# Attention, routed experts and a summed MLP on one core: the sum steps re-spaced, a buffer of its own for the last weights, row turnings inside a y, idle turnings at branches

## Chip, cores and metric

One core of one Trainium2 chip runs the whole program in one launch. The metric is the device time in microseconds (us); the kernel before has a median of 1106.93 us over 3 runs (1106.44 to 1108.24).

## What is computed

Three stages follow each other, all in float32. Each large product is made as three products of a high and a low part (hi·hi, hi·lo, lo·hi).

```python
def reference(**kwargs):
    attn_out = _attn_ref(**attn_kwargs)              # softmax inside chunks of 64
    x = ...reshape(B * S, H * D)                     # 4608 tokens x 512
    x = _moe_ref(x=x, **moe_kwargs)
    return _moe2_ref(x=x, **moe2_kwargs)

# _moe_ref: a token with x @ w_skip > 0 goes to the expert e_idx = argmax(x @ w_gate):
    h = np.maximum(xc[mask] @ w1[e], 0.0)            # 512 -> 1024
    y[mask] = gate_w[mask, None] * (h @ w2[e])       # 1024 -> 512
    out[do_compute] = xc + y

# _moe2_ref: on all tokens
    h = np.maximum(np.maximum(x @ w1, x @ w2), x @ w3)   # 512 -> 768, three times
    return (h @ w_out).astype(np.float32)
```

The weights of the last MLP come in 64-bit words and are narrowed on the chip.

## The kernel before

**Stages.** Attention and routing fill the first 225 us or so. Then come the eight experts `e0` to `e7`, about 225 to 530 us, and then the second MLP in five blocks of tokens (block 0 from about 530 to 660 us, the others to the end).

**An expert.** Tokens are gathered in tiles of 128. `first_tiles` does two tiles together: four groups of `h` products on TensorE (PE), each followed by a high part `hhi` on ScalarE (ACT) and a low part `hlo` on VectorE (DVE), then transposes `trm` of rows that are needed later (ACT writes `xhi`, DVE writes `xlo`), and two `second` calls, whose 24 `y` products each end in `put_back`: DVE adds to `xg` (L694) and GpSimd (POOL) scatters the rows into `x_dram` (L696). A third tile is done by `single`, under a branch on the expert's count (L983); a fourth one stands under a further branch (L916), and more of them in a loop (L920, L921). Expert 0 always does its third tile, and expert 7 does its own (`7_2`) after the branch of L989, before the second MLP. Every engine takes each branch for itself, in its own order of instructions. Where a branch is not taken, the engine makes up the semaphore counts that the skipped instructions would have given, and it does so only after its own earlier work; the others wait for those counts. In the profiled run the branches of `e2`, `e3` and `e5` are taken, and inside them the fourth-tile branches of `e2` and `e3`; those of `e1`, `e4`, `e6` and `e7` are not taken, and neither are the ones after `0_2` and `5_2` and the loops after `2_3` and `3_3`.

**Expert weights.** While expert e runs, the weights of e+1 are loaded on SyncE's queue (SP), split by ACT (`whi_e`) and DVE or POOL (`wlo_e`), and the pieces numbered 6, 4 and 5 are split after the branch.

**Sum steps.** The second MLP uses sums of quarters of its weights in the manner of Strassen, seven products in place of eight. 18 `sums_ahead` steps (#0 to #17) make these sums: 11 of them among the experts, 7 in block 0. A step loads `n_raw`, narrows it into `n_q` (DVE L531, L532, L533, L536, and a square on ACT, L534), forms four sums (DVE L569 to L572), makes the high part on ACT (L575) and the low part on DVE (L576), and stores both to `m_sums` (L577 on ACT's queue, L578 on SP's). Among the experts `n_q` has one buffer, so the next step's first instructions on DVE and ACT wait until the last store has landed. `STEPS` says how many steps stand in each expert: 2, 2, 2, 2, 2, 1, 0, 0. In `first_tiles` they are bound to the first and second group of `h`; in expert 0 they come after the third tile's rows have been turned.

**The seam.** `single("7_2")` calls `sums_T(0, 0)` ahead of its y products. It turns the x rows of block 0 (PE `trf`, L879), which ACT and DVE make into `x_b` and `t` (L884, L885, L890, L893 to L900). These rows are loaded at the start of that stage by `load_first`, on SP, behind every scatter.

**Block 0.** `unit` does seven products of six matmuls each (`f_a`, `f_b`, `f_d`); ACT copies some to `p` and `u`, DVE adds and takes maxima (L1034, L1036, L1056). Each of the first seven of the nine units carries a sum step, and the units 6, 7 and 8 each narrow two halves of the last weights (`m2_direct`, tiles `raw_m` and `n_q_m`, five DVE instructions each). `n_q_m` takes turns with the steps' `n_q` in the two buffers of the tag `s4`. A later unit reads a step's stored sums through `ws` loads (L851).

**Order.** Tile's scheduler sets the order on each engine. It follows the order of the code, dependencies, and `issue_after`, which holds an instruction back in the order behind another one.

## Time and profile before

| what | value |
|---|---|
| median of 3 runs | 1106.93 us (1106.44 to 1108.24) |
| the profiled execution's own time | 1109.83 us |
| its span | 1108.1 us |
| PE busy | 1042.2 us, 94% |
| DVE busy | 614.8 us, 55% |
| ACT busy | 446.2 us, 40% |
| POOL busy | 309.1 us, 28% |
| mean granted clock of PE | 0.979 |

The profiled execution is 2.9 us above the median, and 1.7 us of it lie outside the span. Times in rows count from the span's start. A granted clock of 1.00 is 2.4 GHz and 0.50 is 1.2 GHz. In a timeline, a row's bracket holds the idle time before the instruction and what ended it. A releaser with a q (`DVEq`, `PEq`) is that engine's sequencer: here the counts that it makes up at a branch.

### The profile page before, as it was taken

How to read it: one execution, taken by the hardware profiler on the slowest of the kernel's cores; microseconds unless marked ns; L12 is line 12 of the kernel's file. 1: busy time of each engine (PE TensorE's matmuls, PEld its weight loads, DVE VectorE, ACT ScalarE, POOL GpSimd, SP SyncE). 2: the span in 40 equal slices, each digit the busy share in tenths (PEclk: the TensorE clock that was granted, in tenths of full speed). 3: DMA queues.
4: the chain of work that ended last, by engine and by line, in shares of the span. 5: the costliest groups of instructions: out<-in, count | busy, mean ns of one | idle time of the engine just before them, and what ended most of it. 6: DMA issues, size and time to landing. Idle time of an engine off the chain costs nothing.

```text
span 1108.1 us, 17499 instructions
## 1 busy us (share of the span) xinstructions
PE 1042.2 (94%) x6320; PEld 872.1 (79%) x6320; DVE 614.8 (55%) x1299; ACT 446.2 (40%) x774; POOL 309.1 (28%) x297
## 2 busy tenths in 40 slices
PE   7899799988899998998899799999999999999997
PEld 6788677777788787887687588878888888788996
DVE  6687588756756477671499772335244442443241
ACT  6677487434434244431444342222322232223231
POOL 4124232364404044320432160222312140123021
PEclk9999799999899999999999999999999999999999
DMA  9999996257764468544898934663566545666591
GB/s 211 195 216 232 261 229 183 89 195 259 265 217 136 138 211 273 192 150 141 274 319 285 300 114 136 197 190 114 165 194 192 166 139 166 183 186 208 186 288 38
DMA packets 217513, 216.99 MB, mean 196 GB/s; under 512 B 50219, under 2 KB 179403, under 8 KB 217408
## 3 DMA queue, kind: packets, MB, share of 16 engines
q1 hardware_dynamic: 206384, 183.62, 57.3%
q0 software_dynamic: 8432, 23.76, 6.6%
q10 hardware_dynamic: 2592, 8.26, 1.9%
q8 instruction: 60, 0.98, 0.4%
q14 instruction: 45, 0.37, 0.1%
HBM read 175.15 MB, written 41.83 MB: 196 GB/s over the span
## 4 chain that ended last, share of the span: by engine, by line
PE 41%; DMA 6%; DVE 3%; issue 3%; POOL 1%; ACT 0%; SPq 0%; POOLq 0%; DVEq 0%; ACTq 0%
PE f_a L705 5%; PE f_a L707 5%; PE f_a L706 5%; PE o L705 4%; PE o L707 4%; PE o L706 4%; DMA ws<-m_sums 3%; PE f_d L705 3%; PE f_d L707 3%; PE f_d L706 3%; DMA m_sums<-n_q 2%; PE f_b L705 1%; PE f_b L707 1%; PE f_b L706 1%; PE trf L879 1%
## 5 line engine op out<-in xcount | busy, mean ns | idle before, releaser
L91 POOL TENSOR_TENSOR fh<-best,fh 128x512 fp32r<-128x512 f32 (+1 forms) x60 | 77.0, 1290 | 356.3 <-ACT fh L90 270.4
L705 PE MATMUL f_a<-x_t,ws 128*128 128x512 f32 (+1 forms) x270 | 100.7, 373 | 5.0 <-DVE p L1034 4.8
L706 PE MATMUL f_a<-x_t,ws 128*128 128x512 f32 (+1 forms) x270 | 99.9, 370 | 0.0
L707 PE MATMUL f_a<-x_t,ws 128*128 128x512 f32 (+1 forms) x270 | 99.7, 370 | 0.0
L90 ACT CAST whi_e<-raw_e 128x1024 fp32r<-128x1024 f32 x64 | 65.1, 1045 | 60.0 <-DMA raw_e<-in_moe_w_dram 34.8
L705 PE MATMUL h<-xhi,whi_e 128*128 128x256 f32 x256 | 75.5, 295 | 12.2 <-DVEq L983 7.0
L706 PE MATMUL o<-wlo_m,fh 128*128 128x512 f32 x216 | 84.6, 392 | 0.0
L705 PE MATMUL o<-whi_m,fh 128*128 128x512 f32 x216 | 83.4, 392 | 0.0
L707 PE MATMUL o<-whi_m,fh 128*128 128x512 f32 x216 | 83.4, 392 | 0.0
L91 DVE TENSOR_TENSOR wlo_e<-raw_e,whi_e 128x1024 fp32r<-128x1024 f32 x50 | 67.1, 1351 | 18.1 <-ACT whi_e L90 15.9
L705 PE MATMUL y<-whi_e,hhi 128*128 128x512 f32 x184 | 74.3, 406 | 2.6 <-ACT hhi L772 1.8
L707 PE MATMUL y<-whi_e,hlo 128*128 128x512 f32 x184 | 72.8, 400 | 1.8 <-DVE hlo L712 1.6
L706 PE MATMUL h<-xlo,whi_e 128*128 128x256 f32 x256 | 74.4, 291 | 0.0
L707 PE MATMUL h<-xhi,wlo_e 128*128 128x256 f32 x256 | 74.3, 290 | 0.0
L706 PE MATMUL y<-wlo_e,hhi 128*128 128x512 f32 x184 | 72.3, 395 | 0.0
L696 POOL DMA_INDIRECT x_dram<-xg,ids_sb x20 | 20.6, 1030 | 180.2 <-DVE xg L694 72.8
L90 ACT CAST fh<-best 128x512 fp32r<-128x512 f32 (+1 forms) x60 | 34.7, 579 | 89.5 <-DVE best L1036 57.9
L1039 ACT COPY p<-f_a 128x512 f32<-128x512 f32 (+1 forms) x45 | 24.5, 545 | 99.3 <-PE f_a L707 99.1
L705 PEld LDWEIGHTS h<-xhi,whi_e 128*128 128x128 f32 x256 | 51.0, 199 | 15.3 <-ACTq L983 6.3
L705 PEld LDWEIGHTS f_a<-x_t,ws 128*128 128x128 f32 x270 | 51.2, 190 | 14.5 <-DVE p L1034 5.3
L707 PEld LDWEIGHTS f_a<-x_t,ws 128*128 128x128 f32 x270 | 51.2, 190 | 8.6
L706 PEld LDWEIGHTS f_a<-x_t,ws 128*128 128x128 f32 x270 | 51.2, 190 | 8.3
(226 smaller groups left out, 2678.7 us busy)
## 6 DMA issues: line engine op xcount, KB each, us to landing
ws<-m_sums SPq DMA_DIRECT2D x135, 512.0 KB, 5.2
raw_e<-in_moe_w_dram SPq DMA_DIRECT2D x64, 512.0 KB, 5.1
ws<-m_sums SPq DMA_DIRECT2D x45, 256.0 KB, 3.9
v_bd<-in_v_dram SPq DMA_DIRECT2D x144, 64.0 KB, 4.2
x<-x_dram SPq DMA_DIRECT2D x36, 256.0 KB, 4.9
out_dram<-os SPq DMA_DIRECT2D x36, 256.0 KB, 2.0
x_dram<-xg SPq DMA_DIRECT2D x17, 512.0 KB, 4.2
m_sums<-n_raw ACTq DMA_DIRECT2D x18, 448.0 KB, 6.0
```

The lines of the kernel that those rows point to most:

```text
L90: nc.scalar.copy(hi, src),
L91: eng.tensor_tensor(lo, src, hi.bitcast(F32), op=ALU.subtract),
L696: ins = nc.gpsimd.indirect_dma_start(out=x_dram[:, :], out_offset=bass.IndirectOffsetOnAxis(ap=ids, axis=0), in_=xg, in_offset=None, bound ...
L705: nc.tensor.matmul(acc, ahi, bhi, start=first, stop=False, skip_group_check=onto)
L706: nc.tensor.matmul(acc, ahi, blo, start=False, stop=False, skip_group_check=onto)
L707: return nc.tensor.matmul(acc, alo, bhi, start=False, stop=last, skip_group_check=onto)
L879: nc.tensor.transpose(tr[:, i * P:(i + 1) * P], row[:, c * P:(c + 1) * P], ident)
L1039: nc.scalar.copy(p1, acc_a)
```

## The change

It has four parts.

1. Sum steps: `STEPS` becomes 1, 2, 2, 2, 2, 2, 0, 0, and the two steps of an expert are bound to the first and the third group of `h` in place of the first and the second.
2. Own buffer: `n_q_m` gets a buffer of its own (4 KB per partition), and the first half piece of the last weights goes from unit 6 to unit 3 (`SPREAD`).
3. Seam: `sums_T(0, 0)` is placed behind the third group of the last y (nine of its 24 products). Inside `sums_T`, the split of b22 stands ahead of t2 and t3.
4. Idle turnings: `second` issues eight 128x128 transposes of the identity, into a tile `busy` that nobody reads, behind the last y of a branch's predecessor: after `first_tiles` of e1 to e7, and after every `single` but `7_2`.

```diff
-    def second(name, key, hhi, hlo, i, xg, ids, tag=None):
+    def second(name, key, hhi, hlo, i, xg, ids, tag=None, inside=None, ahead_of_branch=False):
...
-                mm3(acc, hhi[:, kf, sl], hlo[:, kf, sl], bhi[:, kf % 2, :], blo[:, kf % 2, :], n == 0, n == 7)
+                done = mm3(acc, hhi[:, kf, sl], hlo[:, kf, sl], bhi[:, kf % 2, :], blo[:, kf % 2, :], n == 0, n == 7)
+            if inside and n == 2:
+                with tc.issue_after(done.ins):
+                    inside()
+        if ahead_of_branch:
+            busy = ps_tr(f"busy_{name}")
+            with tc.issue_after(done.ins):
+                for n in range(8):
+                    nc.tensor.transpose(busy[:, n % 4 * P:n % 4 * P + P], ident, ident)
         put_back(key, xg, ids, acc)
...
-            if n % 2 == 2 - per and side:
+            if n in (0, 4) and side:
                 with tc.issue_after(done[0].ins), tc.issue_after(done[1].ins):
                     side.pop(0)()
...
-            second(f"{name}_{i}", (e, i), hhi, hlo, i, xgs[i], idss[i], "tr" if e == 0 else None)
+            second(f"{name}_{i}", (e, i), hhi, hlo, i, xgs[i], idss[i], "tr" if e == 0 else None,
+                ahead_of_branch=e > 0 and i == 1)
...
-        second(name, key, hhi, hlo, 0, xg, ids)
+        second(name, key, hhi, hlo, 0, xg, ids, inside=inside, ahead_of_branch=inside is None)
...
-    STEPS = [2, 2, 2, 2, 2, 1, 0, 0]
+    STEPS = [1, 2, 2, 2, 2, 2, 0, 0]
...
-        quarters = four_kb([P, 8, P], F32, f"n_q_m{m}_{f}_{half}", True)
+        quarters = fpool.tile([P, 8, P], F32, tag="n_q_m", name=f"n_q_m{m}_{f}_{half}", bufs=1)
...
         tr22 = turned(cc + 2, 1)
+        split_x("b22", tr22, nc.vector)
         nc.vector.tensor_tensor(t2, tr22, t1, op=ALU.subtract)
         nc.vector.tensor_tensor(t3, tr22, b12, op=ALU.subtract)
-        split_x("b22", tr22, nc.vector)
...
-                single(f"{e}_2", (e, 2), *third, lambda: sums_T(0, 0))
+                single(f"{e}_2", (e, 2), *third, inside=lambda: sums_T(0, 0))
...
+        SPREAD = [0, 0, 0, 1, 0, 0, 1, 2, 2]
...
-                if b == 0 and 3 * f + m >= 6:
-                    for _ in range(min(2, len(rest))):
-                        rest.pop(0)()
+                for _ in range(SPREAD[3 * f + m] if b == 0 else 0):
+                    rest.pop(0)()
```

In the order that is built, DVE reaches the branch after `0_2` (L916 before, L925 now) straight behind `put_back`'s add; the three instructions L531 to L533 of step #1 that stood there before are now in expert 1.

**Place 1: DVE in expert 1, from the first group's `hlo` on.** `n_q_3965` (before) and `n_q_4583` (now) are step #1, `n_q_4572` and `n_q_4653` step #2, `hlo` is one group's low part each, `wlo_e` a piece of the next expert's weights. Before:

```order
L712 SCALAR_TENSOR_TENSOR hlo_4542<-h_0_4543,hhi_4541 128x512
L572 TENSOR_TENSOR n_q_3965<-n_q_3965 128x128
L712 SCALAR_TENSOR_TENSOR hlo_4542<-h_2_4586,hhi_4541 128x512
L91 TENSOR_TENSOR wlo_e_2_4526<-raw_e_2_4523,whi_e_2_4525 128x1024
L576 TENSOR_TENSOR n_q_3965<-n_q_3965,n_raw_3963 128x896
L712 SCALAR_TENSOR_TENSOR hlo_4542<-h_4_4629,hhi_4541 128x512
L91 TENSOR_TENSOR wlo_e_3_4532<-raw_e_3_4529,whi_e_3_4531 128x1024
L712 SCALAR_TENSOR_TENSOR hlo_4542<-h_6_4656,hhi_4541 128x512
```

Now:

```order
L712 SCALAR_TENSOR_TENSOR hlo_4553<-h_4_4624,hhi_4552 128x512
L571 TENSOR_TENSOR n_q_4583<-n_q_4583 128x128
L572 TENSOR_TENSOR n_q_4583<-n_q_4583 128x128
L91 TENSOR_TENSOR wlo_e_3_4543<-raw_e_3_4540,whi_e_3_4542 128x1024
L712 SCALAR_TENSOR_TENSOR hlo_4553<-h_6_4667,hhi_4552 128x512
L576 TENSOR_TENSOR n_q_4583<-n_q_4583,n_raw_4581 128x896
L518 TENSOR_TENSOR xlo_2_4701<-trm_2_0_4702,xhi_2_4700 128x512
```

The low part of step #1 (L576), whose store frees `n_q`, stood ahead of the third group's `hlo` and now stands behind the fourth's. Step #2 follows it in both, behind three `xlo`, and the branch (L983, now L992) behind step #2.

**Place 2: PE at the last y, `7_2`.** `y_2` is its product, `trf_0_1` and `trf_0_0` are the first turnings of block 0's rows. Before:

```order
L770 MATMUL trh_2_0_8229<-ident,h_2_0s 128x128 x4
L705 MATMUL y_2_8278<-whi_e_7_7251,hhi_2_8190 128x512
L706 MATMUL y_2_8278<-wlo_e_7_7252,hhi_2_8190 128x512
L879 MATMUL trf_0_1_8239<-ident,x_1_8173 128x128
L879 MATMUL trf_0_0_8245<-ident,x_0_8172 128x128 x4
L707 MATMUL y_2_8278<-whi_e_7_7251,hlo_2_8191 128x512
```

Now:

```order
L779 MATMUL trh_2_0_8508<-ident,h_2_0s 128x128 x4
L705 MATMUL y_2_8515<-whi_e_7_7458,hhi_2_8469 128x512
L706 MATMUL y_2_8515<-wlo_e_7_7459,hhi_2_8469 128x512
L707 MATMUL y_2_8515<-whi_e_7_7458,hlo_2_8470 128x512
...
L707 MATMUL y_2_8515<-whi_e_6_7964,hlo_2_8470 128x512
L888 MATMUL trf_0_1_8528<-ident,x_1_8452 128x128
L888 MATMUL trf_0_0_8534<-ident,x_0_8451 128x128 x4
L705 MATMUL y_2_8515<-whi_e_6_7964,hhi_2_8469 128x512
```

The five turnings stood behind two of the 24 products of `y_2` and now stand behind nine. Further on, six matmuls of `f` that stood behind the turnings `trf_1_0` now stand ahead of them.

**Place 3: DVE in block 0, between unit 5 and unit 6.** `n_q_8921` (before) and `n_q_9212` (now) are the last sum step, #17; `n_q_m_0_0` and `n_q_m_0_1` are the first two half pieces of the last weights; `best` is the running maximum. Before:

```order
L1034 TENSOR_TENSOR best_0_2_1_8911<-u_0_0_2_8908,f_0_2_d 128x512
L571 TENSOR_TENSOR n_q_8921<-n_q_8921 128x128
L1056 TENSOR_TENSOR best_0_1_2_8655<-best_0_1_2_8655,f_2_1_a 128x512
L572 TENSOR_TENSOR n_q_8921<-n_q_8921 128x128
L531 TENSOR_SCALAR n_q_m_0_0_8981<-raw_m_0_0_8979 128x512
L576 TENSOR_TENSOR n_q_8921<-n_q_8921,n_raw_8825 128x896
```

Now:

```order
L572 TENSOR_TENSOR n_q_9212<-n_q_9212 128x128
L1043 TENSOR_TENSOR p_0_2_1_9108<-p_0_2_1_9108,f_2_1_a 128x512
L1045 TENSOR_TENSOR best_0_1_3_8935<-best_0_1_3_8935,p_0_2_1_9108 128x512
L531 TENSOR_SCALAR n_q_m_0_1_9270<-raw_m_0_1_9268 128x512
L576 TENSOR_TENSOR n_q_9212<-n_q_9212,n_raw_9116 128x896
L1043 TENSOR_TENSOR best_0_2_0_9201<-p_0_0_2_9198,f_0_2_b 128x512
```

The last step's low part (L576) stood behind three sums of unit 6 and behind the first narrowing into a shared buffer. It now stands ahead of unit 6's sums, and the narrowing ahead of it writes into a buffer of its own; the first half piece has gone further up, among unit 4's sums.

## Rows read from the trace of the kernel before

**Rows 1.** The page's part 1: busy us, share of the span, instructions.

```profile
PE 1042.2 (94%) x6320; PEld 872.1 (79%) x6320; DVE 614.8 (55%) x1299; ACT 446.2 (40%) x774; POOL 309.1 (28%) x297
```

**Rows 2.** PE's waits from 225 us on: us in total, times, longest us.

```profile
PE h L705 <- DVEq L983: 7.0, 3, 3.8
...
PE y L707 <- DVE hlo L712: 1.6, 1, 1.6
...
PE h L705 <- PEq L920: 0.8, 1, 0.8
...
PE h L705 <- PEq L916: 0.5, 1, 0.5
```

**Rows 3.** Stretches: start:end, length, PE busy (matmuls), granted clock, DMA share, GB/s.

```profile
262.54:265.95 3.41, 3.41 (x18) 0.50 0.26 78
289.84:296.67 6.83, 6.08 (x28) 0.50 0.98 311
440.03:443.44 3.41, 2.94 (x7) 0.50 1.00 358
521.95:525.36 3.41, 3.41 (x11) 0.50 1.04 342
535.60:539.01 3.41, 3.41 (x12) 0.50 0.18 57
620.94:624.35 3.41, 2.93 (x6) 0.50 0.86 253
0.00:18.00 18.00, 11.52 (x85) 1.00 0.93 217
```

**Rows 4.** Timeline of PE at the branch after `0_2`: start, length, instruction, idle before.

```profile
261.30 0.39 PE L705 MATMUL h<-xhi,whi_e 128*128 128x256 f32 x1 [2.81 <-ACTq L916]
```

**Rows 5.** Timeline of ACT at the same place.

```profile
260.14 0.67 ACT L534 ACTIVATE n_q<-n_raw 128x512 f32<-128x512 f32 x1 [6.07 <-DMA m_sums<-n_q]
```

**Rows 6.** Timeline of DVE in expert 1.

```profile
273.30 1.08 DVE L576 TENSOR_TENSOR n_q<-n_q,n_raw 128x896 fp32r<-128x896 f32 x1
...
283.19 0.43 DVE L531 TENSOR_SCALAR n_q<-n_raw 128x512 int32<-128x512 int32 x1 [1.61 <-DMA m_sums<-n_q]
...
289.52 0.74 DVE L694 SCALAR_TENSOR_TENSOR xg<-y,xg 128x512 f32<-128x512 f32 x1
```

**Rows 7.** The tile `m_sums` from 225 to 530 us: its transfers.

```profile
DMA to landing us min/median/max: 2.5/6.8/9.1
```

**Rows 8.** Timeline of PE in expert 2: transposes, and the taken branch L983.

```profile
304.84 1.47 PE L514 MATMUL trm<-ident,xg 128*128 128x128 f32 x12
...
317.06 0.39 PE L705 MATMUL h<-whi_e,xhi 128*128 128x512 f32 x1
```

**Rows 9.** Timeline of DVE at the start of expert 5.

```profile
426.34 0.43 DVE L531 TENSOR_SCALAR n_q<-n_raw 128x512 int32<-128x512 int32 x1 [6.28 <-DMA m_sums<-n_q]
```

**Rows 10.** Timeline of PE at the seam.

```profile
521.90 1.27 PE L879 MATMUL trf<-ident,x 128*128 128x128 f32 x5 [1.39 <-DMA x<-x_dram]
...
534.35 0.63 PE L879 MATMUL trf<-ident,x 128*128 128x128 f32 x4 [2.16 <-DVE x_b L885]
...
546.13 0.33 PE L879 MATMUL trf<-ident,x 128*128 128x128 f32 x1 [1.16 <-DMA x<-x_dram]
```

**Rows 11.** Timeline of PE in block 0, at its two gaps.

```profile
621.34 0.80 PE L705 MATMUL f_a<-x_t,ws 128*128 128x512 f32 x1 [4.84 <-DVE p L1034]
...
626.07 0.50 PE L705 MATMUL f_a<-x_b,ws 128*128 128x512 f32 x1 [1.80 <-DMA ws<-m_sums]
```

**Rows 12.** Timeline of DVE ahead of these gaps.

```profile
613.15 1.55 DVE L531 TENSOR_SCALAR n_q_m<-raw_m 128x512 int32<-128x512 int32 x1 [1.90 <-DMA m_sums<-n_q]
614.62 1.08 DVE L576 TENSOR_TENSOR n_q<-n_q,n_raw 128x896 fp32r<-128x896 f32 x1
...
617.14 0.69 DVE L536 SCALAR_TENSOR_TENSOR n_q_m<-n_q_m 128x512 f32<-128x512 f32 x1
```

**Rows 13.** A stretch of block 0: PE, PEld, DVE, ACT, POOL busy, granted clock, DMA.

```profile
580.00:600.00 20.00, 20.00 (x90) 16.57 (x89) 18.54 (x33) 8.24 (x14) 6.18 (x8) 1.00 0.88 306
```

More of the change, by code (lines that the diff above doesn't have):

```diff
@@ L748, in first_tiles, with single @@
         for i in range(2):
-            second(f"{name}_{i}", (e, i), hhi, hlo, i, xgs[i], idss[i], "tr" if e == 0 else None)
+            second(f"{name}_{i}", (e, i), hhi, hlo, i, xgs[i], idss[i], "tr" if e == 0 else None,
+                ahead_of_branch=e > 0 and i == 1)
         return hhi, hlo
-    def single(name, key, xT, xg, ids, between=None):
+    def single(name, key, xT, xg, ids, between=None, inside=None):
         e = key[0]
@@ L1059 @@
         rest = [lambda i=i, half=half: m2_direct(3, i, wpool2, half) for i in range(NS) for half in range(2)]
+        SPREAD = [0, 0, 0, 1, 0, 0, 1, 2, 2]
     else:
         rest = [lambda i=i: m2_piece(3, i, wpool2) for i in range(NS)]
+        SPREAD = [0, 0, 0, 0, 0, 0, 1, 1, 1]
     steps = list(range(AHEAD, 2 * len(UNITS)))
```

## Prediction

> **What bounds the kernel now.** I read the busy times first. TensorE (PE) is busy 94% of the span, VectorE (DVE) 55% [rows 1], so the time is PE's work plus PE's idle time, and nothing else counts unless it opens or closes a gap of PE. The second view is therefore PE's waits from the experts on [rows 2]. There the reader sees branches (`DVEq`, `ACTq`, `PEq`: another engine, or PE itself, comes late to a branch) and some late inputs. Third come the stretches in which PE's granted clock is 0.50, so 1.2 GHz [rows 3]. Each follows an idle time of PE: 2.81 us ahead of the one at 262.54, 1.64 ahead of 440.03, 1.39 ahead of 521.95, 2.16 ahead of 535.60, 4.84 ahead of 620.94. What such a stretch costs: at full clock 90 products of 512 columns take 20.00 us, 0.222 each [rows 13]; at 0.50 seven take 2.94 and six 2.93 [rows 3], 0.42 to 0.49. So a stretch loses 7 × 0.20 = 1.4 to 6 × 0.27 = 1.6 us; the 18 half-wide products at 262.54 lose 3.41 − 18 × 0.111 = 1.4 us. A stretch goes if the gap ahead of it goes: 1.80 us [rows 11] and the 0.8 of the `PEq` gaps [rows 2] have none of their own behind them.
>
> **A. Expert 0 to 2: sum steps.** At the branch after `0_2`, PE waits 2.81 us for ACT's counts [rows 4]; ACT stood 6.07 us in front of step #1's square, until step #0's store had landed [rows 5]. That square is gone from there. What is late next is PE itself: eight turnings and its own drain. Twelve transposes take 1.47 us with the latency of the last in it [rows 8], at most 0.12 each; I take 0.11, so eight are 0.88 us; the drain is 0.5 to 0.8 [rows 2]. The gap becomes about 0.88 + 0.7 = 1.6, a gain of 1.2.
> Expert 1 pays for it. Before, it runs from 261.30 to the `DVEq` gap's end at about 290.6, 29.3 us: L576 of step #1 starts at 12.0 and lasts 1.1, step #2 starts 8.8 later when the store has landed, and DVE is done with it and the last `xg` add 7.1 later, at 290.3 [rows 6]. Now L576 stands behind the fourth `hlo`. With h at full clock (96 half-wide products, 10.7 us) and some 2.2 us for the high part and the cast (an estimate from the other casts' and adds' lengths of 0.7 to 1.1 in these rows) it starts at 12.9. With a landing of 6.8, the median of such stores [rows 7], expert 1 lasts 12.9 + 1.1 + 6.8 + 0.2 + 7.1 + 0.3 = 28.4, a gain of 0.9; with the 8.8 that was seen here 30.4, a loss of 1.1; with 2.5, PE's own end decides, 24.2 of products and 1.6 behind them, a gain of 3.5. I take 0.9, the median. Its stretch at half clock brings nothing more, since DVE sets the end. A = 1.2 + 0.9 = **2.1**, between 0.1 and 4.7.
>
> **B. Expert 5.** DVE stood 6.28 us in front of step #8, which was first in its queue [rows 9]; the pieces of the weights and all `hlo` came late behind it, and PE waited 1.6 us for one of them [rows 2] and ran seven products at half clock behind it (1.4). Step #8 now stands behind the weight pieces and the first `hlo`, so the store has 5 us or more to land beside PE's work. B = **3.0**, its upper end; the lower one is 1.6, if only the wait goes.
>
> **C. Experts 4 and 6.** The branches there wait 7.0 − 3.8 = 3.2 us for DVE in two cases [rows 2]. The last step's low part now stands behind the last `xg` add, in front of the branch, in both; its length is 1.1 us [rows 6]. I take 0.5 for each, as about half of it lies beside the turnings (0.88). C = **−1.0**, between 0 and −4.5 (each gap longer by 1.5, with a half-clock stretch of 1.4 behind one).
>
> **D. Idle turnings.** They run at 13 places of this execution: seven branches after `first_tiles`, and after `0_2`, `2_2`, `2_3`, `3_2`, `3_3` and `5_2`. At the five taken branches PE goes on without a gap (the first product behind the branch of expert 2, at 317.06, has no idle time ahead of it) [rows 8], so each pays 0.88: 4.4. Where PE waits for its own sequencer (0.8 and 0.5) [rows 2] the drain follows the turnings: 2 × 0.88 = 1.8. Behind `3_3` PE waits for the `xg` add, which is 0.7 long [rows 6] and runs beside the turnings; I take 0.5, between 0.2 and 0.9. The others hide in gaps that another engine ends, or are in A. D = **−6.7**; ends: −4.4, if only the taken ones pay, and −11.4, if all 13 do.
> On the clock: the first 18 us of the run, which begin with eleven idle transposes and are mostly transposes of q and k, show 1.00 [rows 3].
> The Trainium skill ("TensorE: Matmul & The Clock Gate", Part 4, PE-mode transpose) says that transposes don't count as PE being busy in the way matmuls do, so that the clock is not released by them. By that rule the turnings buy nothing of the clock, the stretch behind `0_2` could stay and push expert 1's chain 1.4 later, and the sum would be 7.0 instead of 8.4. The first 18 us speak against it, though other products are mixed in there.
>
> **E. Seam.** The five turnings of x rows waited 1.39 us for their rows, until 521.90 [rows 10]. They now stand seven products further on, 7 × 0.222 = 1.6 us, so the wait is covered; the loads themselves are not moved. With it goes the half clock from 521.95, some 1.5. The wait of 2.16 for `x_b` [rows 10]: six matmuls (1.3 us) now come ahead of it, but the work on ACT and DVE that it waits for starts at the same time as before, so PE only gets there earlier; I take 0.7, and 0.8 (half) of the stretch at 535.60. The 1.16 for block 1's rows [rows 10]: its turning stands later; I take 0.6. E = 1.4 + 1.5 + 0.7 + 0.8 + 0.6 = **5.0**, between 1.4 (the first wait alone) and 7.7 (all).
>
> **F. Block 0.** PE waits 4.84 us for DVE and 1.80 us for a `ws` load [rows 11], with a stretch of half clock (1.6) between: 8.2 in all. DVE is at 18.5 of 20 us with a sum step in each unit [rows 13]; a unit is 42 products, 9.3 us, so DVE needs 8.6 of it. A half piece is five instructions of 0.43 to 0.69 [rows 12], 3.2 us. Unit 6 with two pieces and the step: 8.6 + 6.4 = 15.0, 5.7 too much; and DVE stood 1.90 us in front of the shared buffer [rows 12]: 7.6. The gap was 4.84, so 2.8 of slack (products ahead of the sums) took the rest. Now the 1.90 is gone (the buffer is its own and holds no store); unit 3 has 2.5 too much, units 4 and 5 give back 0.7 each, unit 6 has 2.5: 3.6, less 2.8 of slack, leaves 0.8. Units 7 and 8 (8.6 − 4.7 for the step + 6.4 = 10.3) add 1.0 each, as they did. So a gap of 0.8 to 2.8; I take 2.2. Step #17's low part, which started at 614.62 [rows 12] and whose store and load made the 1.80, now comes three sums earlier. F = 8.2 − 2.2 = **6.0**; ends 8.2, and 2.0 if unit 3's 2.5 opens a gap of its own and 3.7 of the old one stay. The POOL scatters that now stand ahead of the branches cost nothing: no wait of PE names POOL [rows 2].
>
> **The sum.** 2.1 + 3.0 − 1.0 − 6.7 + 5.0 + 6.0 = 8.4 us. The profiled execution took 1109.83 and would take 1101.4; it is 2.9 above the median of the runs, none of it in a place that the change touches as far as the rows tell, so from the median: 1106.93 − 8.4 = **1098.5**.
>
> **Rivals.** (1) The stalls move and don't go. DVE's work in block 0 is the same, and the seam's chain on ACT and DVE too; with E and F at their low ends the sum is 2.1 + 3.0 − 1.0 − 6.7 + 1.4 + 2.0 = 0.8, 1106.1. For it: DVE has only 1.5 us of room in 20 [rows 13]. Against: the 1.90 and the 1.39 are waits for single transfers.
> (2) Slower: each run of turnings brings a drain, at taken branches too, because the next work takes the bank that they write. Then each of the 13 places costs 0.88 + 0.8 = 1.7: 21.8 instead of 6.7, a sum of −6.7, 1113.6. It decides from 1.3 us a place on (15.1 of gains and 2.2 of margin, over 13, is 1.33). For it: the two `PEq` gaps are such drains. Against: nothing in [rows 8] shows a drain between transposes and products.
> (3) The turnings hold the clock: the gaps at branches leave no half-clock stretch (one of 6.83 us with 28 products stands behind expert 1 [rows 3]; at full clock these half-wide products take 28 × 0.111 = 3.1 of its 6.08 us, so 3.0 are lost), and the turnings cost only the taken 4.4. The sum is 8.4 + 3.0 + 2.3 = 13.7, 1093.2. For it: the clock of the first 18 us [rows 3]. Against: the gap behind expert 1 stays above 2 us in A, and eight turnings fill 0.88 of it.
>
> **How the numbers follow.** A measurement of this kernel tells 0.2%, 2.2 us, from no change. Forecast 0.57 (1093 to 1104), rival 1 0.20, rival 2 0.11, rival 3 0.12. Faster: the forecast but for 0.02, rival 3, and a quarter of rival 1 (0.05): 0.72. Same: most of rival 1 with 0.01: 0.15. Slower: rival 2 and a little of the others: 0.13. The range leaves out rival 2, and what lies below rival 3: 1090.5 to 1107.5.
>
> **What would show it.** A: the gap behind `0_2` under 2 us, and L576 of step #1 behind the fourth `hlo`; the gap behind expert 1 tells the landing. B: no wait of a y in expert 5, and no half clock there. C: `DVEq` gaps of experts 4 and 6 near 2 us. D: 0.88 between the last y and the next h at taken branches. E: no wait on x rows at 521.9. F: one gap under 3 us near unit 6 and no wait of `n_q_m` for a store. I am wrong if taken branches show more than 1.4 us, if the gap behind expert 1 passes 6 us, or if block 0 still loses over 5 us.

## The result and the profile after

The changed kernel takes 1121.48 us (median of 4 runs, 1119.48 to 1128.41); the kernel before, on the same chip, 1106.68 (4 runs, 1105.66 to 1108.24). The ratio is 1.0144, 95% interval 1.0099 to 1.0189: slower, where 1098.5 was forecast, and outside the range that was given. The profiled execution after took 1119.48 with a span of 1117.8, so the two traces hold 9.7 us of the difference; the other 5 lie in which executions were profiled (3.2 above this median before, 2.0 below it after).

Where the 9.7 went, by four landmarks on PE: the first product of h in expert 0's third tile, of h in `7_2`, of f in unit 1, and of f in block 1. The last row ends with PE's last product.

| stretch | before us | after us | difference |
|---|---|---|---|
| attention, routing and expert 0's first tiles, to `0_2` (not touched) | 241.5 | 243.7 | +2.2 |
| experts, `0_2` to `7_2` | 271.3 | 279.8 | +8.5 |
| seam, `7_2` to unit 1 | 36.3 | 28.6 | −7.7 |
| block 0, unit 1 to block 1 | 121.7 | 130.3 | +8.6 |
| the rest | 430.7 | 428.8 | −1.9 |

The first stretch is the same code in every kernel here and took from 240 to 254 us (251 to 254 in the two jobs on one chip, 240 to 246 in the rest), so ratios below are within a job, and mechanisms are read from the lengths of the other stretches. These come from one profiled execution each and have a spread of their own: the experts are the same code in the kernel before and in four kernels below, and took 271.3 us before and 265.5 to 267.0 in those four. Part 1 of the page after, to set beside [rows 1]:

```profile
PE 1050.6 (94%) x6424; PEld 884.3 (79%) x6424; DVE 619.3 (55%) x1299; ACT 447.1 (40%) x774; POOL 311.1 (28%) x297
```

PE is 8.4 us busier, with 104 instructions more: the turnings. PE's waits from 225 us on, after (us in total, times, longest), beside [rows 2]:

```profile
PE h L705 <- ACTq L992: 11.4, 2, 6.3
PE f_a L705 <- ACT p L1048: 6.3, 1, 6.3
PE f_a L705 <- DVE p L1043: 4.9, 1, 4.9
...
PE h L705 <- PEq L998: 1.8, 1, 1.8
...
PE h L705 <- PEq L992: 1.6, 1, 1.6
```

The wait of a y in expert 5 is gone. The `DVEq` waits, 7.0 us in three, are now `ACTq`, 11.4 in two: 5.09 behind expert 1 and 6.28 behind expert 4. Block 0 has two gaps, of 4.9 and 6.3, neither of them at the old place [rows 11]. Half-clock stretches from the experts on, after (start:end, length, PE busy (matmuls), clock, DMA share, GB/s), to set beside [rows 3]:

```profile
291.70:295.11 3.41, 3.29 (x15) 0.50 0.74 276
428.23:435.06 6.83, 5.60 (x26) 0.50 0.79 271
595.48:598.90 3.42, 3.42 (x8) 0.50 1.07 391
605.72:612.55 6.83, 3.52 (x8) 0.50 0.76 260
```

Each stands at one of these four gaps. (One more, at 243.91 after and 242.06 before, stands ahead of them, behind expert 0's wait for `xhi`.) Those of expert 5, of the seam and behind `0_2` are gone, as forecast; the seam's second one was counted by half.

### The profile page after: what moved, and what is told of

Same layout as the page of the kernel before. It is cut to its first block, busy times and chain, and to the rows that moved or that the text cites. A ratio compares the mean times of both kernels' runs of the same rounds, so it can differ in the third digit from the quotient of the medians.

```text
span 1117.8 us, 17664 instructions
## 1 busy us (share of the span) xinstructions
PE 1050.6 (94%) x6424; PEld 884.3 (79%) x6424; DVE 619.3 (55%) x1299; ACT 447.1 (40%) x774; POOL 311.1 (28%) x297
## 4 chain that ended last, share of the span: by engine, by line
PE 46%; DMA 3%; DVE 1%; issue 1%; ACT 1%; POOL 0%; SPq 0%; POOLq 0%; ACTq 0%; DVEq 0%
PE f_a L705 6%; PE f_a L707 6%; PE f_a L706 6%; PE o L706 4%; PE o L707 4%; PE o L705 4%; PE f_d L705 3%; PE f_d L706 3%; PE f_d L707 3%; DMA ws<-m_sums 2%; PE f_b L707 2%; PE f_b L706 2%; PE f_b L705 2%; PE trf L888 1%; DMA n_raw<-in_moe_w_dram 1%
## 5 line engine op out<-in xcount | busy, mean ns | idle before, releaser
L705 PE MATMUL h<-xhi,whi_e 128*128 128x256 f32 x256 | 75.6, 295 | 15.0 <-ACTq L992 11.4
L91 DVE TENSOR_TENSOR wlo_e<-raw_e,whi_e 128x1024 fp32r<-128x1024 f32 x50 | 60.2, 1218 | 22.4 <-ACT whi_e L90 22.3
```

The costliest lines, as they stand in the source:

```text
L91: eng.tensor_tensor(lo, src, hi.bitcast(F32), op=ALU.subtract),
L705: nc.tensor.matmul(acc, ahi, bhi, start=first, stop=False, skip_group_check=onto)
```

## The experiments

Fourteen kernels in four jobs. A diff is against the changed kernel for the first three, against the kernel before for the fourth, and against the fourth for all others.

### One part undone at a time, and the seam alone

No turnings:

```
-                ahead_of_branch=e > 0 and i == 1)
+                ahead_of_branch=False)
...
-        second(name, key, hhi, hlo, 0, xg, ids, inside=inside, ahead_of_branch=inside is None)
+        second(name, key, hhi, hlo, 0, xg, ids, inside=inside, ahead_of_branch=False)
```

> The changed kernel without the eight idle turnings at the 13 places. Theory (the turnings lie wholly on PE's path, at branches that are not taken too, because PE's own jump follows them): 13 x 0.9 to 1.1 us come back, about 10 to 14 us less than the changed kernel, so 1108 to 1112 us. Rival (they are mostly hidden, only the taken branches pay): 4 to 5 us less, 1116 to 1117. Rival (they hold the clock): no gain or a loss, and more half-clock stretches after the branches.

The last pieces two to a unit in units 6 to 8, as before, with the own buffer kept:

```
-        SPREAD = [0, 0, 0, 1, 0, 0, 1, 2, 2]
+        SPREAD = [0, 0, 0, 0, 0, 0, 2, 2, 2]
```

> The changed kernel with the last weights' half pieces back at units 6, 7 and 8 (two each), their own buffer kept. Theory (the piece at unit 3 takes one of the three raw buffers, so step 16's load is issued late, DVE and ACT stand at its first instructions, and the sums of unit 5 behind them hold PE): the gaps of 4.9 and 6.3 us between unit 4 and unit 6 go, block 0 takes 12 to 17 us less than in the changed kernel, 1105 to 1110 us. Rival (the own buffer or the earlier place of step 17 is to blame): the gaps stay, within 3 us of 1121.5. Rival (DVE's total decides, the stall moves to units 6 to 8): 3 to 6 us less.

The sum steps as before:

```
-            if n in (0, 4) and side:
+            if n % 2 == 2 - per and side:
...
-    STEPS = [1, 2, 2, 2, 2, 2, 0, 0]
+    STEPS = [2, 2, 2, 2, 2, 1, 0, 0]
```

> The changed kernel with the sum steps of the experts placed and bound as before. Theory (the later second step holds DVE and ACT at the branches of experts 1, 4 and 6): the gap behind expert 4 falls from 6.3 to about 2 us, the one behind expert 1 from 5.1 to about 3 to 4, but the 2.8 us behind 0_2 and the waits of y in expert 5 come back; net 0 to 5 us less than 1121.5. Rival (the steps' move is a gain of some 5 us and the loss of expert 4 belongs to the turnings): 3 to 6 us more than 1121.5.

The kernel before with nothing but the seam's two edits:

```
+            if inside and n == 2:
+                with tc.issue_after(done.ins):
+                    inside()
...
+        split_x("b22", tr22, nc.vector)
         nc.vector.tensor_tensor(t2, tr22, t1, op=ALU.subtract)
         nc.vector.tensor_tensor(t3, tr22, b12, op=ALU.subtract)
-        split_x("b22", tr22, nc.vector)
...
-                single(f"{e}_2", (e, 2), *third, lambda: sums_T(0, 0))
+                single(f"{e}_2", (e, 2), *third, inside=lambda: sums_T(0, 0))
```

> The kernel before with the seam part alone: row turnings behind nine products of the last y, b22 split earlier. Theory (the seam's gain of 7.8 us by the marks of PE's products is its own): 1099 to 1101 us, and no wait on x rows at the first turnings. Rival (it only moves the wait, and the first units of block 0 give it back): 1104 to 1107.

| run | us | ratio to before, 95% | experts | seam | block 0 |
|---|---|---|---|---|---|
| undo_busy | 1132.76 | 1.0145 (1.0097 to 1.0193) | 276.3 | 28.9 | 132.3 |
| undo_spread | 1135.64 | 1.0167 (1.0112 to 1.0223) | 285.7 | 28.0 | 125.2 |
| undo_steps | 1127.37 | 1.0100 (1.0064 to 1.0136) | 277.7 | 28.7 | 129.8 |
| seam_alone | 1110.83 | 0.9945 (0.9921 to 0.9970) | 267.0 | 30.2 | 121.3 |

Before is 1116.90 here. Undoing any one part leaves the kernel slow, so at least two parts cost. Of the three theories only that of undo_steps came in its time (0 to 5 us less than the changed kernel; by the ratios 4.9); undo_busy and undo_spread were to give back 10 us and more and gave back nothing. The seam alone beats both kernels. In undo_spread the two gaps of block 0 are gone and that stretch is 5.1 shorter than after, but its experts, whose code is that of the changed kernel, took 285.7 in this profile against 279.8; what made them longer stays open, and its ratio doesn't show the gain. PE's waits in block 0 (550 to 680 us) of undo_spread:

```profile
PE f_a L705 <- DMA ws<-m_sums: 6.0, 2, 3.5
PE f_a L705 <- DVE p L1043: 1.3, 1, 1.3
```

From here each part is put on top of seam_alone, one at a time, since the parts cover one another when they are taken out of the whole.

### The sum steps

Both edits of the steps, and then only the table that moves one step out of expert 0 (the second pair of lines without the first):

```
-            if n % 2 == 2 - per and side:
+            if n in (0, 4) and side:
...
-    STEPS = [2, 2, 2, 2, 2, 1, 0, 0]
+    STEPS = [1, 2, 2, 2, 2, 2, 0, 0]
```

> The kernel before with the seam part and the sum steps moved as in the change; no idle turnings. Theory (the second step of an expert waits for the first's store, which now leaves 2 to 5 us later, and DVE and ACT reach the branch behind it): gaps of 5 to 8 us behind experts 1 and 4, and the stretch from the third tile of expert 0 to the last single tile is 7 to 11 us longer than in seam_alone. Rival (in the changed kernel the turnings made these gaps): within 3 us of seam_alone.

> The kernel before with the seam part and the new numbers of steps per expert (1, 2, 2, 2, 2, 2), the binding to the first and second group kept. Theory (taking step #1 out of expert 0 makes every expert finish two whole steps before its branch, and that is the loss; the binding matters little): within 2 us of steps_moved, with gaps of 5 to 9 us behind experts 1 and 4. Rival (the second step's place half an expert later is the loss): 5 us or more shorter than steps_moved, with the gap behind expert 4 under 3 us.

Then both edits with the store of the first steps' low part reading the high part instead, so that no store holds the tile `n_q`; the low parts of these steps don't reach `m_sums`. And the same store in seam_alone, as the control:

```
... seven.rearrange("p n w -> p (n w)"))
... seven.rearrange("p n w -> p (n w)") if i >= AHEAD else hi.bitcast(F32).rearrange("p n w -> p (n w)"))
```

> steps_moved, but the second store of an expert's sum step takes its bytes from the raw tile (the high parts a second time) and not from n_q, so that n_q is free as soon as DVE is done with it; the same bytes move, and the low parts of eleven steps are left out of the sums. Theory (the landing of the first step's store makes the second step late at the branch): the gaps behind experts 1 and 4 fall from 5.0 and 8.6 us to under 2.5, and the stretch from the third tile of expert 0 to the last single tile is 6 to 10 us shorter than in steps_moved. Rival (DVE's and ACT's own work ahead of the branch is too long, or the load of the step's raw words is late): gaps over 4 us stay.

> seam_alone with the same change of the store's source, as a control: the steps stand as before the change. Theory: the gap behind expert 1 (4.4 us in seam_alone) falls under 2.5 and the wait of a y in expert 5 goes, 3 to 6 us less than seam_alone in that stretch. Rival (the landing matters only where the steps were moved): within 1 us of seam_alone.

| run | us | ratio to before, 95% | experts | gaps behind experts 1 and 4 |
|---|---|---|---|---|
| seam_alone (from above) | | 0.9945 | 267.0 | 4.45, 1.78 |
| steps_moved | 1119.04 | 1.0017 (0.9982 to 1.0052) | 275.3 | 4.98, 8.60 |
| steps_count | 1107.47 | 1.0014 (0.9994 to 1.0034) | 275.0 | 5.05, 7.84 |
| steps_store_free | 1099.51 | 0.9945 (0.9919 to 0.9970) | 268.7 | 4.01, 6.42 |
| seam_store_free | 1099.95 | 0.9947 (0.9921 to 0.9973) | 268.4 | 2.79, 4.05 |

Before is 1117.19, 1107.17 and 1105.34 in the three jobs. The steps cost 0.7%, about 8 us, and steps_count shows what in them: not their place within an expert but their number per expert. Freed from the stores, the loss is gone, while the stores themselves cost seam_alone nothing. So the loss needs the landings: waiting for one in the middle of an expert. But the gaps were to fall under 2.5 in both of these kernels and didn't. Of the 6.6 us by which the experts of steps_store_free are shorter than those of steps_moved, 3.2 lie at the two gaps, and beside seam_store_free the gaps are still 1.2 and 2.4 longer, while the stretch as a whole is within 0.3. PE's waits at this branch from 250 to 535 us in seam_alone, steps_moved and steps_store_free, a fence each:

```profile
PE h L705 <- DVEq L986: 5.9, 2, 4.5
```

```profile
PE h L705 <- ACTq L986: 13.6, 2, 8.6
```

```profile
PE h L705 <- ACTq L986: 10.4, 2, 6.4
```

The long gaps shrink but stay. Expert 4 of the changed kernel shows why; timeline (start, length, instruction, idle before) of DVE, then of ACT, POOL and PE:

```profile
400.13 0.42 DVE L531 TENSOR_SCALAR n_q<-n_raw 128x512 int32<-128x512 int32 x1
...
408.48 5.00 DVE L572 TENSOR_TENSOR n_q<-n_q 128x128 f32<-128x128 f32 x1
414.54 1.09 DVE L576 TENSOR_TENSOR n_q<-n_q,n_raw 128x896 fp32r<-128x896 f32 x1 [1.07 <-ACT n_raw L575]
...
422.35 0.43 DVE L531 TENSOR_SCALAR n_q<-n_raw 128x512 int32<-128x512 int32 x1 [2.06 <-DMA m_sums<-n_q]
...
427.66 1.09 DVE L576 TENSOR_TENSOR n_q<-n_q,n_raw 128x896 fp32r<-128x896 f32 x1 [0.39 <-ACT n_raw L575]
```

```profile
413.57 0.94 ACT L575 CAST n_raw<-n_q 128x896 fp32r<-128x896 f32 x1 [5.73 <-DVE n_q L572]
...
422.34 0.70 ACT L534 ACTIVATE n_q<-n_raw 128x512 f32<-128x512 f32 x1 [4.00 <-DMA m_sums<-n_q]
```

```profile
408.59 4.73 POOL L91 TENSOR_TENSOR wlo_e<-raw_e,whi_e 128x1024 fp32r<-128x1024 f32 x2
```

```profile
429.46 0.58 PE L705 MATMUL h<-xhi,whi_e 128*128 128x256 f32 x1 [6.28 <-ACTq L992]
```

The expert holds two whole steps. The first is held up by 5 us: L572, which lasts 0.28 elsewhere, takes 5.00 while POOL makes its two pieces of the next expert's weights, and ACT's cast waits for it. That step ends at 415.63, its store lands 6.7 later, the second step needs 6.4 (422.35 to 428.75), and only then are ACT and DVE at the branch. In seam_alone the expert's last step begins at 412.80, 10.2 behind the expert's first h (in the changed kernel 24.0 behind it), with only one step's end ahead of it; POOL's pair hits it too (L532), but it has 16 us until the next h, and the next step stands behind the branch. DVE in seam_alone, expert 4:

```profile
404.87 1.09 DVE L576 TENSOR_TENSOR n_q<-n_q,n_raw 128x896 fp32r<-128x896 f32 x1 [0.36 <-ACT n_raw L575]
...
412.80 0.42 DVE L531 TENSOR_SCALAR n_q<-n_raw 128x512 int32<-128x512 int32 x1
413.25 5.78 DVE L532 SCALAR_TENSOR_TENSOR n_q<-n_raw,n_q 128x512 int32<-128x512 int32 x1
```

In steps_moved and steps_count the first step of expert 4 is hit in its L576 (5.53 and 5.56 us), so its store goes out later still, and the gaps are the longest. In steps_store_free no landing is waited for, but L572 takes 4.82 again, and ACT's cast of that step stands behind a cast that waited for its weights:

```profile
411.81 1.06 ACT L90 CAST whi_e<-raw_e 128x1024 fp32r<-128x1024 f32 x1 [5.00 <-DMA raw_e<-in_moe_w_dram]
412.77 0.94 ACT L575 CAST n_raw<-n_q 128x896 fp32r<-128x896 f32 x1
```

The second step then begins at 416.24 and ends at 422.64; the h follows at 423.50, after a gap of 6.42. POOL's pair was not taken away in any run, so its share of the loss is read from these rows alone.

### The turnings

Eight turnings behind each last y, on top of seam_alone; then the same ahead of the last three products of that y; then sixteen (`range(16)`) behind it:

```
...
+        if ahead_of_branch:
+            busy = ps_tr(f"busy_{name}")
+            with tc.issue_after(done.ins):
+                for j in range(8):
+                    nc.tensor.transpose(busy[:, j % 4 * P:j % 4 * P + P], ident, ident)
...
+                ahead_of_branch=e > 0 and i == 1)
...
+        second(name, key, hhi, hlo, 0, xg, ids, inside=inside, ahead_of_branch=inside is None)
```

> The kernel before with the seam part and the eight idle turnings behind the last y, as in the change; steps and block 0 as before. Theory (they lie on PE's path at all 13 places, and at branches not taken PE's own jump comes behind them): from the third tile of expert 0 to the last single tile 8 to 11 us longer than in seam_alone, and the idle time behind the turnings of experts 4, 6 and 7 still 1.5 us or more, put down to PE's sequencer. Rival (8 x 0.11 us at the taken branches alone): 4 to 5 us longer.

> As busy_late, with the same eight turnings ahead of the last three products of that y in place of behind them. Theory (behind a branch that is not taken PE needs a fixed time from the last work ahead of the branch that its sequencer can hide behind long products but not behind short turnings): the idle time behind experts 4, 6 and 7 falls to that of seam_alone or less, and the stretch is 2 to 4 us shorter than in busy_late. Rival (the turnings' own time is all they cost): within 1 us of busy_late.

> As busy_late with sixteen turnings in place of eight at each place. Theory (each turning costs its own 0.06 to 0.11 us and hides nowhere): 13 x 0.5 to 0.9, so 7 to 12 us more than busy_late. Rival (a fixed cost per place, such as a drain or a jump): 1 to 4 us more.

| run | us | ratio to before, 95% | experts |
|---|---|---|---|
| busy_late | 1105.56 | 0.9980 (0.9960 to 1.0001) | 275.4 |
| busy_early | 1112.61 | 1.0065 (1.0038 to 1.0092) | 280.4 |
| busy_double | 1121.32 | 1.0144 (1.0101 to 1.0187) | 287.4 |

By the ratios eight turnings cost 0.35%, some 4 us, and sixteen 2.0%, some 22 us. In the profiles the experts are 8.4 and 20.4 longer than those of seam_alone. The 8.4 is made of two parts: from the last y to the next h the thirteen places take 12.2 more, and the work between them takes 3.9 less. Of the 3.9, 2.8 are in expert 5, which waits for a low part in seam_alone; other kernels without turnings lack this wait too. busy_early was to be 2 to 4 us shorter than busy_late and is 5.0 longer; its order differs around expert 4 too, where it has a gap of 6.67 us for ACT, so it doesn't settle what the place alone does.

At a taken branch the turnings cost their own time. Expert 2 with eight (after), then with sixteen (busy_double):

```profile
317.09 1.04 PE L732 MATMUL busy<-ident 128*128 128x128 f32 x8
317.88 0.48 PE L705 MATMUL h<-whi_e,xhi 128*128 128x512 f32 x1
```

```profile
312.16 1.91 PE L732 MATMUL busy<-ident 128*128 128x128 f32 x16
313.82 0.48 PE L705 MATMUL h<-whi_e,xhi 128*128 128x512 f32 x1
```

The next h starts 0.79 behind the first of eight and 1.66 behind the first of sixteen, with no idle time: 0.11 a turning.

At a branch that isn't taken there is more to it. PE at the branch behind expert 6, seam_alone (ahead of it the last product of y), and then after:

```profile
494.43 0.39 PE L707 MATMUL y<-whi_e,hlo 128*128 128x512 f32 x1
496.29 0.36 PE L705 MATMUL h<-xhi,whi_e 128*128 128x256 f32 x1 [1.47 <-DVEq L986]
```

```profile
494.91 0.39 PE L707 MATMUL y<-whi_e,hlo 128*128 128x512 f32 x1
495.14 1.04 PE L732 MATMUL busy<-ident 128*128 128x128 f32 x8
497.77 0.35 PE L705 MATMUL h<-xhi,whi_e 128*128 128x256 f32 x1 [1.60 <-PEq L992]
```

Without turnings 1.86 us pass from the last y to the next h, with an idle time of 1.47 that DVE ends. With them 2.86 pass, and the idle time is still there, 1.60, now ended by PE's own sequencer. It is another wait. PE's own branch instruction stands in the profile too (under PEld; ns, then the start in us), seam_alone, then after:

```profile
L986 PEldq COMPARE_BRANCH  x1: 318/318/318, 492.0 to 492.0; - x1
```

```profile
L992 PEldq COMPARE_BRANCH  x1: 3764/3764/3764, 493.7 to 493.7; - x1
```

In seam_alone PE makes up its counts at 494.9, as soon as its last y is done, and then waits for those of DVE, at 496.1. After, its branch instruction takes 3.76 us in place of 0.32, so PE's counts come at 497.6, 1.4 behind the last turning and 0.6 behind DVE's. In that time, from 493.6 to 497.5, there is one transfer on the queue that the page calls "instruction", of 16 KB:

```profile
q8 instruction: 1, 0.02, 1.9%
```

In the experts of all 16 traces 60 of PE's branch instructions have such a transfer in them, and last 2.3 to 6.7 us; none of the others lasts over 1.9. Those behind experts 6 and 7 have one in all six kernels with turnings (3.3 to 4.9 us), and in none of the ten without (0.32 and 0.41 us). So at these two places PE waits for its own branch, and the turnings make it longer: seam_alone and busy_late, and the changed kernel and undo_busy, differ in them alone. That they do it by shifting the code behind them, and the transfers with it, is likely but not shown, since no run shifts code without turnings. It can go the other way: with sixteen turnings the branch behind expert 1 has no transfer and lasts 0.41 (5.01 with eight), and the gap there is 1.41 (4.26 with eight).

Of the 12.2 us of busy_late, 4.0 are at the five taken branches, 2.2 behind `2_3`, `3_3` and `5_2`, 1.4 behind `0_2` and expert 1, and 4.7 behind experts 4, 6 and 7. At these last three PE's own branch ends last, each with a transfer in it; behind expert 4 it has one in seam_alone too.

### Block 0

The new table alone, the pieces still in the shared buffer; then the same with the first piece's raw words in a buffer of their own, outside the ring of three; then the own buffer of the narrowing without the table:

```
+    SPREAD = [0, 0, 0, 1, 0, 0, 1, 2, 2]
...
-                if b == 0 and 3 * f + m >= 6:
-                    for _ in range(min(2, len(rest))):
-                        rest.pop(0)()
+                for _ in range(SPREAD[3 * f + m] if b == 0 else 0):
+                    rest.pop(0)()
```

> The kernel before with the seam part and the half piece moved to unit 3; the last weights share the steps' buffers as before, and the moved piece's raw words take one of the three raw buffers. Theory (the raw ring is the cause): gaps of 4 to 7 us at units 4 to 6, block 0 (from the start of unit 1 to the end of its outputs) 6 to 12 us longer than in seam_alone. Rival (the loss in block 0 needs the own buffer of the last weights): block 0 within 2 us of seam_alone.

```
-        raw = rpool.tile([P, 1024], I32, tag="raw", name=f"raw_m{m}_{f}_{half}")
+        raw = (fpool if (f, half) == (0, 0) else rpool).tile([P, 1024], I32, tag="raw_m0" if (f, half) == (0, 0) else "raw", name=f"raw_m{m}_{f}_{half}", bufs=1 if (f, half) == (0, 0) else 3)
```

> As spread_ring, but the moved piece's raw words have a buffer of their own, so that the steps keep all three. Theory (raw ring): the gaps at units 4 to 6 are gone, block 0 is 6 to 12 us shorter than in spread_ring and 0 to 4 us shorter than in seam_alone, whose gap at unit 7 is eased. Rival (3 us more of DVE's work in unit 3 is the cause): the gaps stay, within 2 us of spread_ring.

```
-        quarters = four_kb([P, 8, P], F32, f"n_q_m{m}_{f}_{half}", True)
+        quarters = fpool.tile([P, 8, P], F32, tag="n_q_m", name=f"n_q_m{m}_{f}_{half}", bufs=1)
```

> The kernel before with the seam part and the own buffer for the last weights, nothing moved to unit 3. Theory: DVE's 1.9 us wait for a store goes, block 0 is 2 to 5 us shorter than in seam_alone. Rival (undo_spread showed that the own buffer lets the pieces crowd ahead of the last step, and the sums' loads come late): block 0 is 2 to 5 us longer, with a wait for ws loads of over 2 us.

| run | us | ratio to before, 95% | block 0 |
|---|---|---|---|
| seam_alone (from above) | | 0.9945 | 121.3 |
| spread_ring | 1126.29 | 1.0087 (1.0055 to 1.0118) | 136.7 |
| spread_own_raw | 1118.11 | 1.0007 (0.9968 to 1.0045) | 129.0 |
| own_buffer | 1114.92 | 0.9990 (0.9957 to 1.0024) | 125.0 |

The early piece costs 15.4 us with the shared buffer, and 7.7 of it are the ring: the early piece takes one of three raw buffers, and a sum step's load then waits for another. The load of step #16 in seam_alone, on POOL:

```profile
587.05 0.71 POOL L547 DMA_DIRECT2D n_raw<-in_moe_w_dram  x1 [2.66 <-DMA m_sums<-n_raw]
```

In the changed kernel, the loads of steps #16 and #17 on POOL, then ACT, then PE around unit 5:

```profile
594.83 0.72 POOL L547 DMA_DIRECT2D n_raw<-in_moe_w_dram  x1 [0.58 <-DMA m_sums<-n_raw]
598.90 0.72 POOL L547 DMA_DIRECT2D n_raw<-in_moe_w_dram  x1 [3.35 <-DVE n_q_m L533]
```

```profile
601.67 0.69 ACT L534 ACTIVATE n_q<-n_raw 128x512 f32<-128x512 f32 x1 [8.39 <-DMA n_raw<-in_moe_w_dram]
```

```profile
595.39 0.74 PE L705 MATMUL f_a<-x_t,ws 128*128 128x512 f32 x1 [4.94 <-DVE p L1043]
...
609.03 0.80 PE L705 MATMUL f_a<-x_t,ws 128*128 128x512 f32 x1 [6.27 <-ACT p L1048]
```

In seam_alone step #16 gets the buffer that step #13's store has freed. Here the piece's load takes that one, at 587.66, and step #16 waits for the next store to land: its load goes out at 594.83 and has landed at 601.6, so ACT stands 8.39 us in front of that step's square. (Step #17 then waits for the piece itself: 598.90, when DVE has read its raw words, L533 of `n_q_m`.) The sums of unit 5 are queued behind the step, and PE behind them, at 609.03. The gap at 595.39 comes before that; ahead of it DVE had stood 2.06 us for a store's landing, and its cause isn't followed further. With the raw words apart, waits of another kind remain; PE's waits from 550 to 680 us of spread_own_raw:

```profile
PE f_a L705 <- DMA ws<-m_sums: 4.7, 1, 4.7
PE f_a L705 <- ACT u L1048: 2.5, 1, 2.5
PE f_a L705 <- DVE p L1037: 2.2, 2, 1.4
PE f_a L705 <- DVE best L1037: 1.7, 1, 1.7
```

There ACT stands in front of the piece's square until the store out of the shared buffer has landed:

```profile
587.08 0.67 ACT L534 ACTIVATE n_q_m<-raw_m 128x512 f32<-128x512 f32 x1 [7.67 <-DMA m_sums<-n_q]
```

The 1.90 us wait of [rows 12] is gone in seam_alone already, by another order on DVE: the last step's low part starts at 615.07, the first narrowing at 616.67. Block 0 is only 0.4 shorter there, and the gap for DVE is still 4.7. own_buffer is 3.7 longer than seam_alone, with DVE at the last step and PE's waits so:

```profile
616.83 1.08 DVE L576 TENSOR_TENSOR n_q<-n_q,n_raw 128x896 fp32r<-128x896 f32 x1
```

```profile
PE f_a L705 <- DVE p L1037: 2.5, 1, 2.5
PE f_a L705 <- DMA ws<-m_sums: 2.0, 1, 2.0
PE f_b L705 <- DVE best L1059: 1.1, 1, 1.1
```

The gap for DVE is smaller (2.5 against 4.84 [rows 11]), as the prediction had it. But the last step's low part starts 3.4 later than in seam_alone, counted from unit 1, with the first piece's narrowing ahead of it, and other waits open for `ws` and `best`. Whether all of the 3.7 comes from this order isn't shown by a run of its own. Part 2 as the change has it, table and own buffer together, was not added to seam_alone either: block 0 of the changed kernel is 9.0 longer than that of seam_alone, and after the seam, the steps and the turnings 0.9% of the changed kernel's 1.44% is left for it, some 10 us, if the parts add up.

## Why the prediction was wrong

**What held.** PE's idle time is what counts, and half-clock stretches go and come with the gaps ahead of them. **B** came, and that expert took 1.4 less although it began in the half clock that expert 4's gap left it. But the wait of a y for a low part there is seen in three of the ten executions that have these steps as before (before, seam_alone, spread_ring) and in none of the six with the steps moved, so part of B may be luck. **E** was too low: forecast 5.0 (1.4 to 7.7), measured 7.7 in the changed kernel and 6.1 alone. The turnings of the x rows wait no longer, and the stretch at 521.95 is gone:

```profile
532.94 0.71 PE L888 MATMUL trf<-ident,x 128*128 128x128 f32 x5
...
539.33 0.66 PE L888 MATMUL trf<-ident,x 128*128 128x128 f32 x4 [0.31 <-DVE t L902]
```

The wait of 2.16 for `x_b` is down to 0.31, of which the prediction had counted on 0.7; the three terms marked as half or a part were nearly whole.

**A, by its step "what is late next is PE itself".** At `0_2` that was right, a gap of 0.41 us there with the turnings ahead of it, and the stretch from `0_2` to expert 1 is 1.6 shorter. But the 2.81 of [rows 4] was partly that one execution's: in seam_alone, spread_ring, spread_own_raw and own_buffer, where these steps are as before, the gap is 1.25 to 1.54, and the stretch 17.1 to 18.1 us against 18.1 after, so no gain is shown there. Expert 1 was to last 28.4 us and lasted 29.9 (before 29.3), with a gap of 5.09 at its end. The step that failed is "it starts at 12.9": L576 started 17.4 behind the first h (261.88), because POOL's pair of weight pieces fell on this step's L533, which I hadn't looked for:

```profile
268.15 5.60 DVE L533 SCALAR_TENSOR_TENSOR n_q<-n_raw,n_q 128x512 int32<-128x512 int32 x1
...
279.27 1.08 DVE L576 TENSOR_TENSOR n_q<-n_q,n_raw 128x896 fp32r<-128x896 f32 x1
```

The landing was then short (4.4 where I took 6.8), which kept the loss small.

**C is the step that failed most in the experts.** "The last step's low part now stands behind the last `xg` add" was priced as 1.1 us of one instruction, half of it beside the turnings: −1.0, −4.5 at worst. What stands there is a chain: a first step whose L572 took 5.00 instead of 0.28, beside POOL's pair, the landing of its store (6.7) and all of the second step (6.4). Expert 4 alone lost 4.95 between the two traces, and the steps as a whole cost 8 on top of seam_alone, where A, B and C were to bring 4.1. The chain from step to store to step was worked out for expert 1, in A; for expert 4 it wasn't, and there it ends last.

**D's sum was near, with one step of it wrong.** Forecast −6.7, ends −4.4 and −11.4; busy_late −8.4 in the experts, some −4 by the ratios. The terms that it counted stand in busy_late: 4.0 at the taken branches for 4.4, 1.7 behind `2_3` and `5_2` for 1.8, 0.5 behind `3_3` for 0.5, at 0.11 a turning. What failed is "the others hide in gaps that another engine ends": behind experts 1, 4, 6 and 7 they cost 5.4, and 4.7 of that where PE's own branch, not another engine, ends the gap. The 3.9 that came back between the branches was not forecast.

**F is the step that failed most of all.** +6.0, ends 8.2 and 2.0; measured −8.6. I counted DVE's arithmetic for each unit, with slack carried over, and said that unit 3 "has 2.5 too much". A piece is also a load into one of three raw buffers, and a place in POOL's and ACT's queues. Neither was counted, so the wait that appeared, 8.39 us for a raw load, isn't in the sum or in its ends. And the 1.90 us that I counted as "gone" brought 0.4 at most where it went alone, in seam_alone.

**The rivals.** Rival 1 (the stalls move, 1106.1) was nearer in kind: they did move, but grew. Rival 2 named the right side with the wrong mechanism: it decides from 1.3 us a place, and a taken branch costs 0.79, the thirteen together 12.2, 0.94 each. Rival 3 isn't borne out as a gain, since turnings cost more than they gave; whether they hold the clock through a short gap stays open, since no run had the gap without its causes. In the whole kernel the turnings partly lie in the gaps that the steps open: seam_alone's 267.0 with 8.4 and 8.3 would be 283.7, and the changed kernel has 279.8. That would be why undoing either part alone gave back 3.5 us or less in its profile; with the spread of such stretches it is argued, not shown (undo_spread, with the same code there, took 285.7).

The price of all that, by the traces: 2.2 (to `0_2`) + 8.5 − 7.7 + 8.6 − 1.9 = 9.7.

## What to carry to other kernels

When a step moves, follow its whole chain to the next branch or sum: the buffer it loads into, the store whose landing frees its tile, the queue that it waits in, and the other engine's work that holds it; a wait that one execution shows in front of it may be what keeps later work in order. Instructions that are put in ahead of a branch can make the branch itself longer, so look at the engine's own branch before and after; and where several parts are changed at once, add each one alone to a common base, since undoing them one by one hides what they cover for each other. Here the seam's two edits alone were worth 0.55%, and no other part added to them gained anything.

## What the runs showed that was not expected

- PE's branch instruction lasts 0.07 to 1.9 us, or 2.3 to 6.7 when a 16 KB transfer of the queue "instruction" lies in it. All six kernels with turnings have such a transfer in the branches behind experts 6 and 7, and none of the ten without. The wait's label, PE's own sequencer, is the only trace of it among PE's waits.
- While POOL makes two pieces of weights (4.73 us in a row, once in each of experts 1 to 6), a DVE instruction that reads SBUF alone lasts until it is done: L572 5.00 instead of 0.28. Where POOL pauses between the two pieces, two DVE instructions share this time (2.94 and 2.78 in expert 5 after). Those that also read a product of PE (L712, L694) keep their 0.7. The Trainium skill ("GPSIMD Engine Reference", 1. Specifications) says that GpSimd's interfaces to SBUF are shared with VectorE, with contention for instructions in a 2-port perf mode or with two SBUF inputs. L572, L533 and L576, with two inputs, agree; L531 has one and lasted 5.68 in expert 2 after, and no row here tells its mode. Where such a pair falls on a chain of steps depends on the order, and so on any edit ahead of it.
- 128x128 transposes of f32 in a row cost 0.11 us each (1.66 less 0.79 us for eight more).
- An untouched stretch of 241 us ahead of `0_2` took 240 to 254 us; that is more than any of the change's parts was worth.
